# Attention with grouped keys: scores computed keys-first, exp read straight from PSUM, row sums checked on the chip

## The chip, the core and the metric

The kernel runs on one core of a Trainium2 chip. The metric is the device time of one execution in microseconds (us). A core has five engines that run their own instruction streams and meet at semaphores: PE (TensorE, matrix multiply; "PEld" is its weight load), DVE (VectorE), ACT (ScalarE), POOL (GpSimd) and SP (SyncE, which here only issues DMAs). Matmuls write to PSUM, 8 banks of 512 f32 values per partition; everything else works in SBUF.

## The reference

```python
B, Hq, Hkv, Sq, Sk, D = 16, 32, 8, 288, 512, 128     # q, k, v: bfloat16, normal * 0.05
k = jnp.repeat(k, rep, axis=1)                        # rep = Hq // Hkv = 4
v = jnp.repeat(v, rep, axis=1)
scores = jnp.einsum("bhqd,bhkd->bhqk", q, k) * D ** -0.5
p = softmax(scores, axis=-1)
out = jnp.einsum("bhqk,bhkd->bhqd", p, v)             # (16, 32, 288, 128) bfloat16
```

Four query heads share one key head, so for each of the 16 x 8 = 128 pairs of batch and key head (a "group" here) there are 4 x 288 = 1152 query rows against the same 512 keys. Inputs are 16.8 MB of k, 16.8 MB of v and 37.7 MB of q; the output has 37.7 MB.

## The kernel before

The 1152 query rows of a group are cut into 9 units of 128 rows; there are 1152 units in all. A unit goes through these steps:

- `op_s` (L229, PE): one matmul, the unit's 128 queries as weights, the group's 512 keys streamed, into one bank of `ps_s` (three banks in turn). Queries lie on partitions, keys along the row.
- `op_dve` (L242, DVE): multiplies the scores by minus the scale into `sn_sb` (f32, SBUF) and takes the row minimum into `nmx_sb`, which is minus the row maximum.
- `op_pool` (L254, POOL): negates and adds that, so that the row maximum becomes 0; the result `x_sb` is bfloat16.
- `op_xt` (L271, PE): four 128 x 128 transposes of `x_sb` into `ps_x` (two units per buffer), so that keys come onto partitions, as the next matmul needs them.
- `op_exp` (L289, ACT): exp of two units at a time, 1024 values per partition, from `ps_x` into `pt_sb` (bfloat16).
- `op_pv` (L315, PE): four matmuls accumulate the unit's output: `pt_sb` as weights, `v_sb` streamed with 129 columns. Column 129 of `v_sb` is ones, so it yields the row sum. Three units share one bank of `ps_o` (two banks in turn).
- `op_rc` (L334, DVE): reciprocals of three row sums, `rl_sb`.
- `op_oev` (L376 on DVE, L385 on ACT): the scaled output of three units to `o_sb`. One in five goes to DVE as one instruction, the others to ACT as three.

The order on each engine is written out by hand: each step of unit u gets a due time (u, u + 1, u + 3 and so on, with lags `LAG_XT` = 3 and `LAG_PV` = 8), and each engine's list is sorted by it. SP issues the DMAs batch by batch (`op_load_qk`, `op_load_v`, `op_store`): a DMA transpose of q, a wait for it, one of k, a wait for it, then v, with two buffers; the first batch is loaded in two halves. The output of a batch is stored with one DMA, that of the last batch in four. In the store each row of 128 values (256 bytes) is a piece of its own, because row c x 128 + p of a group lies on partition p.

Of the kernel before, what the change touches and what calls it, by code (L numbers as in the profile page):

```python
# [6 lines left out]
ACTF = mybir.ActivationFunctionType  # L7
CFG = {}
BF16 = mybir.dt.bfloat16
FP32 = mybir.dt.float32  # L10


def bass_standalone__gqa_softmax__near_ridge_kernel(
# [8 lines left out]
    rep = Hq // Hkv  # L22
    P = 128
    assert D == P and Sk % P == 0 and (rep * Sq) % P == 0
    NJ = Sk // P
    NT = (rep * Sq) // P
    G = Hkv
    NG = B * G
    U = NG * NT
    UPB = G * NT  # L30
    FREE = NJ * P
    assert FREE * 4 <= 2048
    scale = float(D) ** -0.5
    DV = D + 1
    OPB = 2048 // (DV * 4)
    assert OPB >= 1 and NT % OPB == 0

    q_v = q.rearrange("b h s d -> b (h s) d")
    k_v = k.rearrange("b g s d -> b (g s) d")
    o_v = out.rearrange("b h s d -> b (h s) d").rearrange("b (c p) d -> b p c d", p=P)  # L40
    v_v = v.rearrange("b g s d -> b (g s) d").rearrange("b (c p) d -> b p c d", p=P)

    NSB = CFG.get('NSB', 3)
    NXB = CFG.get('NXB', 3)
    NS = CFG.get('NS', 3)
    NX = CFG.get('NX', 4)
    NPB = CFG.get('NPB', 4)
    NM = 8
    NR = 2
    XPB = CFG.get('XPB', 2)  # L50
    assert NS >= NSB and NSB + NXB * ((XPB + 1) // 2) + 2 <= 8
    LAG_XT = CFG.get('LAG_XT', 3.0)
    LAG_PV = CFG.get('LAG_PV', 8.0)
    OE_PERIOD = CFG.get('OE_PERIOD', 5)
    OE_DVE = CFG.get('OE_DVE', (2,))

    n_xc = (U + XPB - 1) // XPB
    n_oc = (U + OPB - 1) // OPB

    def xc_units(c):  # L60
        return list(range(c * XPB, min(U, (c + 1) * XPB)))

    def oc_units(r):
        return list(range(r * OPB, min(U, (r + 1) * OPB)))

    with ExitStack() as es:  # L66
        block = es.enter_context(nc.Block())
        v_sb = es.enter_context(nc.sbuf_tensor("v_sb", [P, 2, G, NJ, DV], BF16))
        o_sb = es.enter_context(nc.sbuf_tensor("o_sb", [P, 2, G, NT, D], BF16))
        qt_sb = es.enter_context(nc.sbuf_tensor("qt_sb", [P, 2, G, NT, P], BF16))  # L70
        kt_sb = es.enter_context(nc.sbuf_tensor("kt_sb", [P, 2, G, NJ, P], BF16))
        scr_sb = es.enter_context(nc.sbuf_tensor("scr_sb", [P, 16], FP32))
        sn_sb = es.enter_context(nc.sbuf_tensor("sn_sb", [P, NS, FREE], FP32))
        x_sb = es.enter_context(nc.sbuf_tensor("x_sb", [P, NX, FREE], BF16))
        pt_sb = es.enter_context(nc.sbuf_tensor("pt_sb", [P, NPB, XPB, NJ, P], BF16))
        nmx_sb = es.enter_context(nc.sbuf_tensor("nmx_sb", [P, NM], FP32))
        rl_sb = es.enter_context(nc.sbuf_tensor("rl_sb", [P, NR, OPB], FP32))
        ident = es.enter_context(nc.sbuf_tensor("ident", [P, P], BF16))
        ones_sb = es.enter_context(nc.sbuf_tensor("ones_sb", [P, P], BF16))
        ps_s = es.enter_context(nc.psum_tensor("ps_s", [P, NSB, FREE], FP32))  # L80
        ps_x = es.enter_context(nc.psum_tensor("ps_x", [P, NXB, XPB, NJ, P], BF16))
        ps_o = es.enter_context(nc.psum_tensor("ps_o", [P, 2, 512], FP32))
        class Chan:

            def __init__(self, name, n):
                self.n = n
                self.sems = [es.enter_context(nc.semaphore("%s%d" % (name, i))) for i in range(n)]

            def w(self, i, mult=1):
                return (self.sems[i % self.n], (i // self.n + 1) * mult)  # L90

            def s(self, i):
                return self.sems[i % self.n]

        c_ldq = Chan("ldq", 2)
        c_ldk = Chan("ldk", 2)
        c_ldv = Chan("ldv", 2)
        c_qkfree = Chan("qkfree", 2)
        c_vfree = Chan("vfree", 2)
        c_out = Chan("outd", 2)  # L100
        c_s = Chan("s", NSB)
        c_dve = Chan("dve", NS)
        c_pool = Chan("pool", max(NS, NX))
        c_xt = Chan("xt", NX)
        c_xc = Chan("xc", NXB)
        c_exp = Chan("exp", max(NPB, NXB))
        c_pv = Chan("pv", max(XPB * (NPB - 1) + 1, OPB + 1))
        c_rc = Chan("rc", NR)
        c_oev = Chan("oev", 2)
        c_osta = Chan("osta", 2)  # L110
        c_ostd = Chan("ostd", 2)
        s_init = es.enter_context(nc.semaphore("s_init"))
        s_q0a = es.enter_context(nc.semaphore("s_q0a"))
        s_pca = [es.enter_context(nc.semaphore("s_pca%d" % i)) for i in range(3)]
        s_pcd = [es.enter_context(nc.semaphore("s_pcd%d" % i)) for i in range(3)]
        s_k0a = es.enter_context(nc.semaphore("s_k0a"))
        s_c0 = es.enter_context(nc.semaphore("s_c0"))

        def emit(eng, waits, fn):
            waits = [(s, n) for (s, n) in waits if n > 0]  # L120
            for (s, n) in waits[:-1]:
                eng.wait_ge(s, n)  # L122
            ins = fn()
            if waits:
                s, n = waits[-1]
                ins.wait_op(s, n, "sem-ge")
            return ins

        def grp_of(u):
            return u // NT  # L130

        def bat_of_group(g):
            return g // G

        pe_pending = []

        def pe_carry(ins):
            if pe_pending:
                ins.then_inc(pe_pending.pop(0), 1)

        sp_plain = []

        def sp_drain():
            for (s, n) in sp_plain:
                nc.sync.wait_ge(s, n)
            del sp_plain[:]

        GH = G // 2 if G >= 2 else 0

        def op_load_qk(b, part=None):  # L150
            eng = nc.sync
            bb = b % 2
            sp_drain()
            if b >= 2:
                eng.wait_ge(*c_qkfree.w(b - 2))
            if part is None:
                g0, g1 = 0, G
            elif part == 0:
                g0, g1 = 0, GH
            else:  # L160
                g0, g1 = GH, G
            sq = s_q0a if part == 0 else c_ldq.s(b)
            sk = s_k0a if part == 0 else c_ldk.s(b)
            nq = 16 if part == 0 else c_ldq.w(b, 16)[1]
            nk = 16 if part == 0 else c_ldk.w(b, 16)[1]
            eng.dma_start_transpose(
                qt_sb[:, bb, g0:g1].rearrange("d g t p -> d (g t p)"),
                q_v[b, g0 * NT * P:g1 * NT * P]).then_inc(sq, 16)
            eng.wait_ge(sq, nq)
            eng.dma_start_transpose(  # L170
                kt_sb[:, bb, g0:g1].rearrange("d g j p -> d (g j p)"),
                k_v[b, g0 * NJ * P:g1 * NJ * P]).then_inc(sk, 16)
            eng.wait_ge(sk, nk)

        def op_load_v(b):
            eng = nc.sync
            bb = b % 2
            if b >= 2:
                eng.wait_ge(*c_vfree.w(b - 2))
            else:  # L180
                eng.wait_ge(s_init, 1)
            eng.dma_start(  # L182
                v_sb[:, bb].rearrange("p g j e -> p (g j) e")[:, :, 0:D], v_v[b]).then_inc(c_ldv.s(b), 16)
            sp_plain.append(c_ldv.w(b, 16))

        NPC = 4 if G % 4 == 0 else 1
        GPP = G // NPC

        def op_store(b, piece=None):
            eng = nc.sync  # L190
            bb = b % 2
            if piece is None or piece == NPC - 1:
                if n_oev_act[b]:
                    eng.wait_ge(*c_osta.w(b))
                if n_oev_dve[b]:
                    eng.wait_ge(*c_ostd.w(b))
            else:
                if piece_has[(False, piece)]:
                    eng.wait_ge(s_pca[piece], 1)
                if piece_has[(True, piece)]:  # L200
                    eng.wait_ge(s_pcd[piece], 1)
            if piece is None:
                g0, g1 = 0, G
            else:
                g0, g1 = piece * GPP, (piece + 1) * GPP
            eng.dma_start(
                o_v[b, :, g0 * NT:g1 * NT],
                o_sb[:, bb, g0:g1].rearrange("p g t d -> p (g t) d")).then_inc(c_out.s(b), 16)
            if piece is None:
                sp_plain.append(c_out.w(b, 16))  # L210

        def op_s(u):
            eng = nc.tensor
            g = grp_of(u)
            b = bat_of_group(g)
            bb = b % 2
            gl = g % G
# [289 lines left out]
```

## Time and profile before

| | |
|---|---|
| time, median of 3 runs | 829.54 us (829.42 to 829.66) |
| profiled execution: span from the first to the last instruction | 828.8 us |
| busy: PE, DVE, ACT, POOL | 96%, 96%, 95%, 94% of the span |
| granted TensorE clock, mean | 0.998 |
| DMA: moved, mean busy share of the 16 DMA engines (queue of SP) | 109.06 MB, 63.5% |
| HBM read and written by the instructions' own account | 16.78 MB and 37.75 MB |

The profile comes from one execution, with a record of each instruction. Its own time is the span, 0.7 us below the median of the runs. "Busy" is the time in which at least one instruction of the engine was in work; matmuls overlap in the records, so the pace of PE is better read from the starts of consecutive matmuls than from their lengths. A group's row has its busy time, the mean length of one instruction in ns, and the idle time of the engine just before such instructions with what ended it.

### The profile page before, as it was taken

The numbers are of one execution on the slowest core, as the hardware profiler recorded it, in microseconds if no ns is written. First come the engines' busy times: TensorE is split into PE (matmuls) and PEld (weight loads), VectorE is DVE, ScalarE is ACT, GpSimd is POOL, SyncE is SP. The second block draws the span as 40 slices with busy tenths as digits, with TensorE's granted clock in tenths as the row PEclk, the third lists the DMA queues.
The fourth block names the chain that finished last, engine by engine and source line by source line (L and its number), as shares of the span: only waits on it lengthen the run. The fifth ranks groups of instructions, "written<-read, shape, count | busy, mean of one in ns | idle before, by whom it ended". The sixth has DMA issues, their size and how long they took to land.

```text
span 828.8 us, 30229 instructions
## 1 busy us (share of the span) xinstructions
PE 791.8 (96%) x10177; PEld 643.5 (78%) x10368; DVE 795.6 (96%) x2786; ACT 786.2 (95%) x1517; POOL 778.9 (94%) x1157
## 2 busy tenths in 40 slices
PE   3999999999999999999999999999999999999996
PEld 1778878878888788778788788787888888787785
DVE  3999999999999999999999999999999999999995
ACT  2999999999999999999999999999999999999997
POOL 3999999999999999999999999999999999999995
PEclk9999999999999999999999999999999999999999
DMA  6868758297691857848387573876919569383522
GB/s 133 162 140 168 167 116 170 51 173 159 116 217 34 184 119 153 181 75 176 85 167 167 114 154 72 172 158 117 214 28 196 115 132 202 85 161 90 116 59 59
DMA packets 378633, 111.00 MB, mean 134 GB/s; under 512 B 362096, under 2 KB 378480, under 8 KB 378480
## 3 DMA queue, kind: packets, MB, share of 16 engines
q1 hardware_dynamic: 378480, 109.06, 63.5%
q8 instruction: 84, 1.38, 0.7%
q14 instruction: 69, 0.57, 0.2%
HBM read 16.78 MB, written 37.75 MB: 66 GB/s over the span
## 4 chain that ended last, share of the span: by engine, by line
PE 41%; ACT 39%; issue 17%; DMA 2%; ACTq 0%; DVE 0%; SPq 0%
ACT o_sb L385 22%; ACT pt_sb L289 17%; PE ps_o L315 15%; PE ps_x L271 14%; PE ps_s L229 11%; DMA v_sb<-in_v_dram 1%; DMA qt_sb<-in_q_dram 1%; DMA kt_sb<-in_k_dram 1%; ACT scr_sb L405 0%; ACTq L66 0%; DVE rl_sb L334 0%; ACTq L122 0%; SPq L182 0%
## 5 line engine op out<-in xcount | busy, mean ns | idle before, releaser
L254 POOL TENSOR_SCALAR x_sb<-sn_sb,nmx_sb 128x512 bf16<-128x512 f32 x1152 | 778.4, 698 | 39.9 <-DVE sn_sb L242 36.1
L242 DVE TENSOR_SCALAR_CACHE_REDUCE sn_sb<-ps_s 128x512 f32<-128x512 f32 x1152 | 756.4, 680 | 23.5 <-PE ps_s L229 22.0
L289 ACT ACTIVATE pt_sb<-ps_x 128x1024 bf16<-128x1024 bf16 x576 | 595.4, 1074 | 35.6 <-PE ps_x L271 27.5
L315 PE MATMUL ps_o<-v_sb,pt_sb 128*128 128x129 bf16 x4608 | 459.5, 221 | 9.4 <-ACT o_sb L385 2.3
L271 PE MATMUL ps_x<-ident,x_sb 128*128 128x128 bf16 x4608 | 445.6, 219 | 10.4 <-POOL x_sb L254 0.2
L271 PEld LDWEIGHTS ps_x<-ident,x_sb 128*128 128x128 bf16 x4608 | 324.9, 97 | 140.8 <-POOL x_sb L254 46.4
L229 PE MATMUL ps_s<-kt_sb,qt_sb 128*128 128x512 bf16 x961 | 363.9, 379 | 12.0 <-DMA kt_sb<-in_k_dram 12.0
L315 PEld LDWEIGHTS ps_o<-v_sb,pt_sb 128*128 128x128 bf16 x4608 | 306.3, 98 | 25.9 <-ACT o_sb L385 20.6
L385 ACT ACTIVATE o_sb<-ps_o,rl_sb 128x128 bf16<-128x128 f32 x921 | 283.3, 413 | 1.2 <-DVE rl_sb L334 1.2
L229 PEld LDWEIGHTS ps_s<-kt_sb,qt_sb 128*128 128x128 bf16 x1152 | 113.4, 98 | 13.1 <-DMA kt_sb<-in_k_dram 12.0
L242 DVE DVE_READ_ACCUMULATOR sn_sb<-ps_s 128x1 f32 x1152 | 95.7, 83 | 0.0
L334 DVE RECIPROCAL rl_sb<-ps_o 128x3 f32<-128x3 f32 x384 | 67.4, 176 | 3.6 <-PE ps_o L315 3.6
L376 DVE TENSOR_TENSOR o_sb<-ps_o,rl_sb 128x384 bf16<-128x384 f32 x77 | 42.6, 553 | 0.0
L405 ACT ACTIVATE scr_sb<-ones_sb 128x1 f32<-128x1 bf16 x16 | 4.3, 271 | 0.0
L289 ACT ACT_TABLE_LOAD x1 | 1.3, 1283 | 1.8 <-POOL ident L443 1.8
L443 POOL TENSOR_SCALAR_AFFINE_SELECT ident<-ones_sb 128x128 bf16<-128x128 bf16 x1 | 0.3, 295 | 0.9 <-DVE v_sb L470 0.9
L469 DVE MEMSET ones_sb<- 128x128 bf16 x1 | 0.2, 165 | 0.9 <-PEq L492 0.9
L403 DVE MEMSET scr_sb<- 128x1 f32 x16 | 0.9, 59 | 0.0
L400 ACT ACTIVATE scr_sb<-ones_sb 128x1 f32<-128x1 bf16 x3 | 0.9, 314 | 0.0
L492 POOL MEMSET const-float32-0.0<- 128x1 f32 x1 | 0.1, 99 | 0.3 <-issue 0.3
L470 DVE MEMSET v_sb<- 128x64 bf16 x1 | 0.1, 112 | 0.2 <-issue 0.2
L398 DVE MEMSET scr_sb<- 128x1 f32 x3 | 0.2, 59 | 0.0
(3 smaller groups left out, 0.3 us busy)
## 6 DMA issues: line engine op xcount, KB each, us to landing
out_dram<-o_sb SPq DMA_DIRECT2D x15, 2304.0 KB, 15.5
out_dram<-o_sb SPq DMA_DIRECT2D x4, 576.0 KB, 3.5
qt_sb<-in_q_dram SPq DMA_TRANSPOSE x17, 12.2
kt_sb<-in_k_dram SPq DMA_TRANSPOSE x17, 6.8
v_sb<-in_v_dram SPq DMA_DIRECT2D x16, 0.2 KB, 7.5
```

What stands on the lines that cost most here:

```text
L229: emit(eng, waits, lambda: eng.matmul(ps_s[:, u % NSB, :], qt_sb[:, bb, gl, t, :], kt_sb[:, bb, gl].rearrange("p j c -> p (j c)"), start=T ...
L242: emit(eng, waits, lambda: eng.tensor_scalar(out=sn_sb[:, u % NS, :], in0=ps_s[:, u % NSB, :], scalar1=-scale, scalar2=None, op0=ALU.mult, ...
L254: emit(eng, waits, lambda: eng.tensor_scalar(out=x_sb[:, u % NX, :], in0=sn_sb[:, u % NS, :], scalar1=-1.0, scalar2=nmx_sb[:, u % NM:u % N ...
L271: ins = emit(eng, w, lambda: eng.transpose(ps_x[:, c % NXB, slot, j, :], x_sb[:, u % NX, j * P:(j + 1) * P], ident[:]))
L289: emit(eng, waits, lambda: eng.activation(pt_sb[:, c % NPB, 0:n].rearrange("p a j c -> p (a j c)"), ps_x[:, c % NXB, 0:n].rearrange("p a j ...
L315: ins = emit(eng, w, lambda: eng.matmul(ps_o[:, r % 2, oslot * DV:(oslot + 1) * DV], pt_sb[:, c % NPB, slot, j, :], v_sb[:, bb, gl, j, :], ...
L334: emit(eng, waits, lambda: eng.reciprocal(rl_sb[:, r % NR, 0:n], src.rearrange("p a e -> p (a e)"))).then_inc(c_rc.s(r), 1)
L376: emit(eng, waits, lambda: eng.tensor_tensor(out=o_sb[:, bb, gl, t0:t0 + n, :], in0=src_o, in1=rl_sb[:, r % NR, 0:n].unsqueeze(2).broadcas ...
L385: ins = emit(eng, w, lambda: eng.activation(o_sb[:, bb, gl, t0 + i, :], ps_o[:, r % 2, i * DV:i * DV + D], ACTF.Identity, scale=rl_sb[:, r ...
L400: nc.scalar.activation(scr_sb[:, 8 + pc:9 + pc], ones_sb[:, 0:1], ACTF.Identity).then_inc(s_pca[pc], 1)
L403: nc.vector.memset(scr_sb[:, b % 2:b % 2 + 1], 0.0).then_inc(c_ostd.s(b), 1)
L405: nc.scalar.activation(scr_sb[:, 4 + b % 2:5 + b % 2], ones_sb[:, 0:1], ACTF.Identity).then_inc(c_osta.s(b), 1)
```

## The change

The kernel is rewritten around chunks. A group's scores are 4 key blocks x 1152 query rows = 4608 columns with 128 keys on the partitions; they are cut into three chunks of 1536 columns, which is three PSUM banks. `ps_s` holds two chunks.

- `op_s(n)`: for chunk n, matmuls with a block of 128 keys as weights and queries streamed; cuts fall at bank borders and at ends of key blocks, so each chunk takes four matmuls (512, 512, 128, 384 columns in the first). The scores come out transposed.
- `op_exp(n)` (ACT): exp of the whole chunk from `ps_s` (f32) to `pt_sb`, with the scale folded in. No row maximum is subtracted.
- `op_pv(r)`: 12 matmuls for three output tiles. Tile t takes the query rows p x 9 + t, so the weights are read from `pt_sb` with a step of 9 elements.
- `op_rc`, `op_ev` (DVE): reciprocals, kept for the whole run in `rl_sb`, and all evictions.
- `op_stat` (DVE): once per batch, largest and smallest reciprocal. At the end these give a flag: 1 or more if a reciprocal is over 2^30 or under 2^-30. A one-column matmul adds the flags of all partitions, and each engine loads the result into a register.
- `general_path`: the old computation (with the row maximum, and evictions on DVE alone), emitted behind a branch that each engine takes if the register isn't zero.
- SP: loads in units of four groups with three slots, k before q, without waits between transposes; the first unit as one group and three. Stores per group, with 9 x 128 values (2304 bytes) in one piece per partition, from six buffers.

```diff
+    CB = 3
+    CH = CB * BANK          # 1536
+    LAG = NC + 1            # NC = 3 chunks a group
+    UG = 4
+    NSLOT = 3
+    NPT = 3
+    NO = 6
+    o_v = out.rearrange("b h s d -> (b h s) d").rearrange("(g p t) d -> g p (t d)", p=P, t=NT)
+        ps_s = main.enter_context(nc.psum_tensor("ps_s", [P, 2, CH], FP32))
+        ps_o = main.enter_context(nc.psum_tensor("ps_o", [P, 2, BANK], FP32))
...
+        def op_s(n):
...
+            if n >= 2:
+                waits.append(("s_e", n - 1))
+            ps = pieces(i)
+            for x, (a, b) in enumerate(ps):
+                j, r0 = a // R, a % R
+                ins = emit(eng, waits if x == 0 else [], lambda: eng.matmul(
+                    ps_s[:, n % 2, a - i * CH:b - i * CH],
+                    kt_sb[:, sl, gi, j * P:(j + 1) * P],
+                    qt_sb[:, sl, gi, r0:r0 + b - a], start=True, stop=True))
+            ins.then_inc(sem["s_s"], 1)
...
+        def op_pv(r):
...
+            waits = [("us_v%d" % sl, 16 * (u // NSLOT + 1)), ("s_e", NC * (g + 1))]
+            if r >= 2:
+                waits.append(("s_ev", r - 1))
+            for a in range(3):
+                t = 3 * (r % NC) + a
+                for j in range(NJ):
+                    w = pt_sb[:, g % NPT, j * R:(j + 1) * R].rearrange("k (p t) -> k t p", t=NT)[:, t]
+                    ins = emit(eng, waits if a == 0 and j == 0 else [], lambda: eng.matmul(
+                        ps_o[:, r % 2, a * DV:(a + 1) * DV], w,
+                        v_sb[:, sl, gi * NJ + j, 0:DV],
+                        start=(j == 0), stop=(j == NJ - 1)))
+            ins.then_inc(sem["s_pv"], 1)
...
+        def op_exp(n):
+            eng = nc.scalar
+            g, i = n // NC, n % NC
+            waits = [("s_s", n + 1)]
+            if g >= NPT:
+                waits.insert(0, ("s_pv", NC * (g - NPT + 1)))
             emit(eng, waits, lambda: eng.activation(
+                pt_sb[:, g % NPT, i * CH:(i + 1) * CH], ps_s[:, n % 2], ACTF.Exp, scale=scale)
+            ).then_inc(sem["s_e"], 1)
...
+        for u in range(1, NU):
+            sp.append((-8.0 if u < NSLOT else NC * UG * (u - NSLOT + 1) + LAG, lambda u=u: op_load(u)))
+        for g in range(NG):
+            sp.append((NC * (g + 1) + LAG + 1.5, lambda g=g: op_store(g)))
...
         @block.tensor
         def _(eng):
+            for n in range(NS + LAG):
+                if n < NS:
+                    op_s(n)
+                if n >= LAG:
+                    op_pv(n - LAG)
+            emit(eng, [("s_bad", 1)], lambda: eng.matmul(
+                ps_s[0:1, 0, 0:1], one_f[:], ck_sb[:, 3:4], start=True, stop=True)
+            ).then_inc(sem["s_bad"], 1)
...
+        def guarded(key, first=None):
+            def body(eng):
+                eng.wait_ge(sem["s_flag"], 1)
+                reg = eng.alloc_register("bad_" + key)
+                eng.load(reg, flag_i[:])
+                with eng.If_ne(reg, 0):
+                    if first:
+                        first(eng)
+                    fns[key](eng)
+            return body
```

More of the change, by code (lines that the diff above doesn't have):

```diff
@@ L48, in bass_standalone__gqa_softmax__near_ridge_kernel @@
[L48 to L64, printed above, removed]
@@ L66, in bass_standalone__gqa_softmax__near_ridge_kernel @@
-    with ExitStack() as es:
-        block = es.enter_context(nc.Block())
[L68 to L117, printed above, removed]
@@ new lines, in bass_standalone__gqa_softmax__near_ridge_kernel, with S, need @@
+    VP = 160
+    LAG = NC + 1
+    UG = 4
+    NU = NG // UG
+    NSLOT = 3
+    NPT = 3
+    NO = 6
+    q_v = q.rearrange("b h s d -> (b h s) d")
+    k_v = k.rearrange("b g s d -> (b g s) d")
+    v_v = v.rearrange("b g (j p) d -> p (b g j) d", p=P)
+    o_v = out.rearrange("b h s d -> (b h s) d").rearrange("(g p t) d -> g p (t d)", p=P, t=NT)
+    with ExitStack() as es:
+        sem = {}
+        def S(name):
+            if name not in sem:
+                sem[name] = es.enter_context(nc.semaphore(name))
+            return sem[name]
+        flag_i = es.enter_context(nc.sbuf_tensor("flag_i", [1, 1], I32))
+        block = es.enter_context(nc.Block())
+        main = ExitStack()
+        v_sb = main.enter_context(nc.sbuf_tensor("v_sb", [P, NSLOT, UG * NJ, VP], BF16))
+        qt_sb = main.enter_context(nc.sbuf_tensor("qt_sb", [P, NSLOT, UG, R], BF16))
+        kt_sb = main.enter_context(nc.sbuf_tensor("kt_sb", [P, NSLOT, UG, Sk], BF16))
+        pt_sb = main.enter_context(nc.sbuf_tensor("pt_sb", [P, NPT, COLS], BF16))
+        o_sb = main.enter_context(nc.sbuf_tensor("o_sb", [P, NO, NT, D], BF16))
+        rl_sb = main.enter_context(nc.sbuf_tensor("rl_sb", [P, NG * NT], FP32))
+        st_sb = main.enter_context(nc.sbuf_tensor("st_sb", [P, 2, B], FP32))
+        ck_sb = main.enter_context(nc.sbuf_tensor("ck_sb", [P, 4], FP32))
+        one_f = main.enter_context(nc.sbuf_tensor("one_f", [P, 1], FP32))
+        dum = main.enter_context(nc.sbuf_tensor("dum", [P, 2], FP32))
+        ps_s = main.enter_context(nc.psum_tensor("ps_s", [P, 2, CH], FP32))
+        ps_o = main.enter_context(nc.psum_tensor("ps_o", [P, 2, BANK], FP32))
+        seen = {}
+        def need(eng, waits):
+            left = []
+            for (s, n) in waits:
+                key = (id(eng), s)
+                if seen.get(key, 0) < n:
+                    seen[key] = n
+                    left.append((sem[s], n))
+            return left
@@ L119, in emit @@
         def emit(eng, waits, fn):
-            waits = [(s, n) for (s, n) in waits if n > 0]
+            waits = need(eng, waits)
             for (s, n) in waits[:-1]:
@@ L175, in op_load_v @@
[L175 to L210, printed above, removed]
@@ L295, in op_pv @@
[L295 to L323 removed]
+                ins.wait_op(waits[-1][0], waits[-1][1], "sem-ge")
@@ new lines, in op_store, with pieces @@
+        def op_store(g):
+            eng = nc.sync
+            for (s, n) in need(eng, [("s_ev", NC * (g + 1))]):
+                eng.wait_ge(s, n)
+            eng.dma_start(o_v[g], o_sb[:, g % NO].rearrange("p t d -> p (t d)")).then_inc(sem["s_o%d" % (g % NO)], 16)
+        def pieces(i):
+            cuts = sorted({i * CH, (i + 1) * CH}
+                          | {x for x in range(0, COLS, BANK) if i * CH < x < (i + 1) * CH}
+                          | {x for x in range(0, COLS, R) if i * CH < x < (i + 1) * CH})
+            return list(zip(cuts[:-1], cuts[1:]))
@@ L329, in op_rc @@
-            waits = []
-            if r >= NR:
-                waits.append(c_oev.w(r - NR))
-            waits.append(c_pv.w(us[-1]))
-            src = ps_o[:, r % 2, 0:n * DV].rearrange("p (a e) -> p a e", e=DV)[:, :, D:DV]
-            emit(eng, waits, lambda: eng.reciprocal(
-                rl_sb[:, r % NR, 0:n], src.rearrange("p a e -> p (a e)"))
-            ).then_inc(c_rc.s(r), 1)
-        obuf_waited = {(False, bq): False for bq in range(B)}
-        obuf_waited.update({(True, bq): False for bq in range(B)})
@@ L437, in bass_standalone__gqa_softmax__near_ridge_kernel @@
[L437 to L448 removed]
+            src = ps_o[:, r % 2, 0:3 * DV].rearrange("p (a e) -> p a e", e=DV)[:, :, D:DV]
@@ new lines, in op_rc, with op_ev @@
+            emit(eng, [("s_pv", r + 1)], lambda: eng.reciprocal(
+                rl_sb[:, 3 * r:3 * r + 3], src.rearrange("p a e -> p (a e)"))
+            ).then_inc(sem["s_rc"], 1)
+        def op_ev(r):
+            eng = nc.vector
+            g = r // NC
+            waits = [("s_rc", r + 1)]
+            if g >= NO:
+                waits.insert(0, ("s_o%d" % (g % NO), 16 * (g // NO)))
+            t0 = 3 * (r % NC)
+            src = ps_o[:, r % 2, 0:3 * DV].rearrange("p (a e) -> p a e", e=DV)[:, :, 0:D]
+            emit(eng, waits, lambda: eng.tensor_tensor(
+                out=o_sb[:, g % NO, t0:t0 + 3, :], in0=src,
+                in1=rl_sb[:, 3 * r:3 * r + 3].unsqueeze(2).broadcast_to([P, 3, D]),
+                op=ALU.mult)).then_inc(sem["s_ev"], 1)
```

621 lines of the change are left out of this document (339 added, 282 removed).

## The prediction

> **What bounds the kernel now.** I read the shares first, then the costliest groups, then the chain of waits, then single stretches of the timeline. The first two rows below are busy time by engine and the granted TensorE clock, the third is the chain that ended last, and the rest are groups (busy us, mean ns of one, idle before).
>
> ```profile
> PE 791.8 (96%) x10177; PEld 643.5 (78%) x10368; DVE 795.6 (96%) x2786; ACT 786.2 (95%) x1517; POOL 778.9 (94%) x1157
> PEclk9999999999999999999999999999999999999999
> PE 41%; ACT 39%; issue 17%; DMA 2%; ACTq 0%; DVE 0%; SPq 0%
> L254 POOL TENSOR_SCALAR x_sb<-sn_sb,nmx_sb 128x512 bf16<-128x512 f32 x1152 | 778.4, 698 | 39.9 <-DVE sn_sb L242 36.1
> L242 DVE TENSOR_SCALAR_CACHE_REDUCE sn_sb<-ps_s 128x512 f32<-128x512 f32 x1152 | 756.4, 680 | 23.5 <-PE ps_s L229 22.0
> L289 ACT ACTIVATE pt_sb<-ps_x 128x1024 bf16<-128x1024 bf16 x576 | 595.4, 1074 | 35.6 <-PE ps_x L271 27.5
> L271 PE MATMUL ps_x<-ident,x_sb 128*128 128x128 bf16 x4608 | 445.6, 219 | 10.4 <-POOL x_sb L254 0.2
> L315 PEld LDWEIGHTS ps_o<-v_sb,pt_sb 128*128 128x128 bf16 x4608 | 306.3, 98 | 25.9 <-ACT o_sb L385 20.6
> L385 ACT ACTIVATE o_sb<-ps_o,rl_sb 128x128 bf16<-128x128 f32 x921 | 283.3, 413 | 1.2 <-DVE rl_sb L334 1.2
> L334 DVE RECIPROCAL rl_sb<-ps_o 128x3 f32<-128x3 f32 x384 | 67.4, 176 | 3.6 <-PE ps_o L315 3.6
> L376 DVE TENSOR_TENSOR o_sb<-ps_o,rl_sb 128x384 bf16<-128x384 f32 x77 | 42.6, 553 | 0.0
> ```
>
> Five engines stand at 94 to 96%: no single one bounds the kernel, and an edit that relieved one would gain nothing. This edit relieves four. So the question is what is left to do per piece, on which engine it is longest, and at what pace. Matmul durations overlap in the records (219 ns each for 128 columns), so I take the pace from start to start. These timeline rows (start, length, engine, line, count) are from a full stretch and from the last one:
>
> ```profile
> 401.70 0.27 PEld L315 LDWEIGHTS ps_o<-v_sb,pt_sb 128*128 128x128 bf16 x4
> 401.75 0.40 PE L315 MATMUL ps_o<-v_sb,pt_sb 128*128 128x129 bf16 x4
> 401.99 0.38 PE L229 MATMUL ps_s<-kt_sb,qt_sb 128*128 128x512 bf16 x1
> 402.20 0.38 PE L271 MATMUL ps_x<-ident,x_sb 128*128 128x128 bf16 x4
> 402.43 0.40 PE L315 MATMUL ps_o<-v_sb,pt_sb 128*128 128x129 bf16 x4
> 822.68 0.88 PE L315 MATMUL ps_o<-v_sb,pt_sb 128*128 128x129 bf16 x12 [1.28 <-ACT o_sb L385]
> 399.77 0.92 ACT L385 ACTIVATE o_sb<-ps_o,rl_sb 128x128 bf16<-128x128 f32 x3
> 400.52 1.99 ACT L289 ACTIVATE pt_sb<-ps_x 128x1024 bf16<-128x1024 bf16 x2
> 402.33 0.96 ACT L385 ACTIVATE o_sb<-ps_o,rl_sb 128x128 bf16<-128x128 f32 x3
> ```
>
> The reader should take four paces from them. One 512-column score matmul: 401.99 to 402.20, 0.215 us. Four transposes: 402.20 to 402.43, 0.23 us, or 57 ns each. Four PV matmuls: 401.75 to 401.99, 0.24 us, about 58 ns each (the run of 12 gives (0.88 - 0.22)/11 = 60 ns). One exp of 1024: two start at 400.52 and the next group starts at 402.33, so 0.905 us; the evictions of 128 go at 0.25 us (399.77 to 400.52 for three). A weight load of 98 ns precedes each matmul, and the pace of 58 ns shows that it is hidden beside the matmuls.
>
> **The change, part by part.** There are 128 groups (batch times key head) of 9 x 128 query rows. After the change each group is three chunks of 1536 score columns (keys on partitions), so 384 chunks.
>
> Removed: DVE's scaling with the row minimum (L242), POOL's subtraction (L254) and the 36 transposes of a group. POOL is left with nothing. DVE keeps the reciprocal and takes all evictions: 384 x (0.176 + 0.553) = 280 us. That is half the time to come, and it runs beside PE with two ps_o banks, so I cost it at nothing; were it not hidden, each chunk would have 0.73 us more.
>
> PE per chunk: four score matmuls with 1536 columns, 3 x 0.215 plus a few ns for the fourth piece = 0.65 us; twelve PV matmuls of 129 columns, 12 x 58 ns = 0.70 us. Sum 1.35 us, 384 x 1.35 = 518 us.
>
> On the Trainium skill's page "TensorE: Matmul & The Clock Gate" (Back-to-back issue gap) the sustained pace of a load-and-matmul stream at 128 columns is about 81 ns. The trace's 58 ns contradicts it for contiguous weights; with 81 ns the chunk would be 0.65 + 0.97 = 1.62 us and the whole some 645 us.
>
> ACT per chunk: one exp of 1536 from PSUM instead of 1.5 of 1024, and no evictions. Its cost is not in the trace. From below: the step between 128 and 1024 elements, (0.905 - 0.25)/896 = 0.73 ns an element (too low, as the eviction also reads a per-row scale), gives 0.905 + 512 x 0.73 ns = 1.28 us. From above: proportional, 0.905 x 1.5 = 1.36 us. I take 1.32, the middle: 507 us. Reading f32 in place of bf16 from PSUM I cost at nothing, since the eviction reads f32. PE is thus longest by a hair.
>
> Does the new ring of waits hold the two back? Score chunk n+2 waits until exp n has emptied its half of ps_s, exp n+2 waits for score chunk n+2. One round: exp (1.32 plus the 0.17 by which a 1.07 record exceeds its pace) + scores 0.65 + matmul drain 0.16 (0.38 - 0.215) = 2.30 us plus two signals, against 2 x 1.35 = 2.70 for two chunks. About 0.2 us per signal is spare, so the ring is not the bound, but jitter will cost something. I put 1% on the steady part (5 us): the kernel before loses 4% of PE with five engines level, here two or three are.
>
> Weights of PV: they are now read with a step of 9 elements (18 bytes) in pt_sb, because query row p x 9 + t goes to partition p. No row of this trace has a stepped weight read. From below nothing (still hidden under 58 ns), from above the full recorded 98 ns without any cover: 12 x 98 = 1.18 us. I take nothing, as today's loads of 98 ns hide in a 58 ns pace; the upper end is a rival below.
>
> Start. These rows are the issue times on SP's queue and, from the chain in order of time, the landings:
>
> ```profile
> 0.80 4.75 SPq L166 DMA_TRANSPOSE qt_sb<-in_q_dram  x1
> 0.80 6.85 DMA qt_sb<-in_q_dram
> 7.66 2.01 SPq L170 DMA_TRANSPOSE kt_sb<-in_k_dram  x1
> 7.66 4.32 DMA kt_sb<-in_k_dram
> 12.06 7.66 DMA v_sb<-in_v_dram
> 12.03 2.01 PE L229 MATMUL ps_s<-kt_sb,qt_sb 128*128 128x512 bf16 x4 [12.03 <-DMA kt_sb<-in_k_dram]
> ```
>
> Issuing takes 1.0 ns a row (4608 rows in 4.75, 2048 in 2.01), landing 2.2 us more. The new first load is one group: 512 + 1152 rows, not waited for in between: 0.8 + 0.5 + 1.2 + 2.2 = 4.7 us to the first matmul, where it was 12.0. Then three groups more (5.1 us of issue) and V, half of the 1 MB that took 7.66 us: about 12.5 us until the first PV. By then PE can do five score chunks (3.2 us), so it idles 12.5 - 4.7 - 3.2 = 4.6 us.
>
> Loads and stores otherwise: a load of four groups now waits on SP for the PV of the slot's former owner, and stores queue behind it; they wait about 7 us of issue, and six o_sb buffers (6 x 4.05 us) cover that. Stores become one row of 2304 bytes per partition where they were 256-byte pieces. The DMA rows:
>
> ```profile
> q1 hardware_dynamic: 378480, 109.06, 63.5%
> out_dram<-o_sb SPq DMA_DIRECT2D x15, 2304.0 KB, 15.5
> out_dram<-o_sb SPq DMA_DIRECT2D x4, 576.0 KB, 3.5
> qt_sb<-in_q_dram SPq DMA_TRANSPOSE x17, 12.2
> kt_sb<-in_k_dram SPq DMA_TRANSPOSE x17, 6.8
> 364.00:378.00 14.00, 13.73 (x180) 10.70 (x184) 13.79 (x51) 13.88 (x30) 13.62 (x21) 1.00 0.92 170
> 385.00:401.00 16.00, 15.71 (x207) 12.87 (x209) 15.74 (x55) 15.79 (x33) 15.50 (x24) 1.00 0.98 216
> ```
>
> The transfers keep the 16 engines busy for 0.635 x 828.8 = 526 us. If stores of the new shape cost what they do now, DMA needs as long as PE; if they cost half, 526 - 16 x 15.5/2 = 402 us. I take the cheaper end, since each partition's piece is nine times as long, and cost DMA at nothing. The cover is thin: DMA then works 80% of the time.
>
> End. After the last exp three PV chunks remain, part of the 518 but behind a wait of about 0.4 us. The rest of the tail:
>
> ```profile
> 823.60 0.18 DVE L334 RECIPROCAL rl_sb<-ps_o 128x3 f32<-128x3 f32 x1 [1.38 <-PE ps_o L315]
> 821.65 0.56 DVE L376 TENSOR_TENSOR o_sb<-ps_o,rl_sb 128x384 bf16<-128x384 f32 x1
> 824.81 0.37 SPq L206 DMA_DIRECT2D out_dram<-o_sb  x1
> ```
>
> Reciprocal, eviction and two signals 1.2 us; the last store, half of the 576 KB that take 3.5 us, about 3. The check of the row sums (32 small reductions of DVE during the run, hidden; then two more, two tiny operations, a one-column matmul, a copy) runs beside the store. What follows does not: every engine waits for the flag, loads a register and jumps over the other program. No row shows a register load or a long jump; from below 0.2 us (what stands after the last landing now), from above, by the nearest fetches from memory, two landings of 3.5 us. I take 3.
>
> Sum: 4.7 + 4.6 + 518 + 5 + 0.4 + 1.2 + 3 + 3 = 540 us of span, where the profiled execution has 828.8; the median of the runs, 829.54, lies 0.7 above that span, so 541 us.
>
> **The rivals.** (1) *Stepped weights are no longer hidden.* For it: each of the 128 reads of a partition jumps 18 bytes; every load row before is contiguous. Against: nothing in rows. At 98 ns per PV matmul the chunk is 0.65 + 1.18 = 1.83 us: 384 x 1.83 + 22 = 725 us; at half way (78 ns) 632 us. The Trainium skill speaks for it: "SBUF — State Buffer" (Door 1, on cachelines) has lines of 16 bytes that need two hits each for full bandwidth, and 18 bytes never hit twice. It also speaks against: "TensorE: Matmul & The Clock Gate" (Weight-path perf modes) allows the fast load a column step up to 1024 elements. No run here shows either yet.
>
> (2) *The other side: slower than before.* The same place, but the load takes twice its present record and nothing covers it: 2 x 98 = 196 ns, chunk 3.0 us, some 1174 us. It decides from (829.5 - 22)/384 - 0.65 = 1.45 us for twelve, 121 ns per PV matmul.
>
> (3) *DMA becomes the bound.* For it: 526 us as they stand, and engines were busy only 0.92 to 0.98 of a stretch full of transfers. Unchanged stores give 526/0.95 + 12 = 566 us, with score matmuls waiting for kt_sb and qt_sb. Against: the long store rows, and loads issued some 20 chunks (27 us) ahead.
>
> (4) *The other program runs as well.* If the sums left the allowed range (2^-30 to 2^30), the old computation would follow: about 541 + 850 = 1390 us. The inputs are normal numbers times 0.05, so scores are near 0 and sums near 512. I give it under 1%.
>
> **How the numbers follow.** Forecast (PE pace, 524 to 560): 0.55. DMA bound (545 to 590): 0.14. Stepped weights (1), anywhere from 570 to 760: 0.26, of which a third is above 680. Slower, (2) and (4): 0.04. The remaining 0.01 is around no change; 0.2% is about what a measurement of this kernel can tell from no change. The low end 524 is paces at their floor (1.32 us a chunk, 507 + 17). The high end 680 leaves 0.04 + 0.09 + a few hundredths out. Faster 0.95, same 0.01, slower 0.04.
>
> **What would show it.** PE near 95%, ACT near 94%, POOL empty, DVE about half; three-chunk rhythm of 4.05 us a group; score matmuls still 0.215 us apart, PV 58 ns apart. If PV starts lie 70 ns or more apart while ACT idles behind PE, (1) is right. If PE's idle time ends with kt_sb or qt_sb landings and the DMA share is above 0.95, (3). If exp takes over 1.36 us from start to start, ACT is the bound and I mis-sized it. First matmul at about 5 us; the time from the last eviction's end to the end about 6 us.

## The result and the profile after

The changed kernel takes 542.37 us (542.26 to 542.77, 4 runs) against 829.56 us before on the same chip: a ratio of 0.6539, 95% interval 0.653 to 0.6548. The profiled execution spans 540.5 us. These are rows of its page: busy time by engine, the chain that ended last by engine, the costliest groups, the DMA queue and the stores.

```profile
PE 526.1 (97%) x6146; PEld 427.7 (79%) x6146; DVE 289.8 (54%) x808; ACT 523.3 (97%) x386; POOL 0.2 (0%) x4
PE 96%; DMA 1%; SPq 1%; DVE 1%; issue 0%
L460 ACT ACTIVATE pt_sb<-ps_s 128x1536 bf16<-128x1536 f32 x384 | 521.9, 1450 | 5.9 <-PE ps_s L429 5.8
L447 PEld LDWEIGHTS ps_o<-v_sb,pt_sb 128*128 128x128 bf16 x4608 | 333.2, 140 | 40.4 <-DMA v_sb<-in_v_dram 0.6
L429 PE MATMUL ps_s<-qt_sb,kt_sb 128*128 128x512 bf16 (+3 forms) x1536 | 315.2, 328 | 7.2 <-DMA qt_sb<-in_q_dram 7.0
L480 DVE TENSOR_TENSOR o_sb<-ps_o,rl_sb 128x384 bf16<-128x384 f32 x384 | 214.1, 557 | 13.5 <-DVE rl_sb L468 0.3
L468 DVE RECIPROCAL rl_sb<-ps_o 128x3 f32<-128x3 f32 x384 | 69.3, 181 | 230.8 <-PE ps_o L447 230.8
q1 hardware_dynamic: 299584, 109.07, 87.0%
out_dram<-o_sb SPq DMA_DIRECT2D x128, 288.0 KB, 4.3
```

POOL is empty and DVE is at half, as forecast. PE and ACT both stand at 97%, so the shares do not tell which of them sets the pace. The chain names PE (96%), but it also does so, with 95%, for a run below that goes at ACT's pace, so it does not decide either. The page also has a sign of the disputed step: a PV weight load is recorded with 140 ns, where the same load had 98 ns before. The rhythm is in the timeline of PE (start, length, engine, line, count):

```profile
300.16 0.81 PE L429 MATMUL ps_s<-qt_sb,kt_sb 128*128 128x384 bf16 x4
300.81 0.86 PE L447 MATMUL ps_o<-v_sb,pt_sb 128*128 128x129 bf16 x12
301.50 0.81 PE L429 MATMUL ps_s<-qt_sb,kt_sb 128*128 128x512 bf16 x4
302.15 0.86 PE L447 MATMUL ps_o<-v_sb,pt_sb 128*128 128x129 bf16 x12
302.85 0.81 PE L429 MATMUL ps_s<-qt_sb,kt_sb 128*128 128x512 bf16 x4
303.50 0.90 PE L447 MATMUL ps_o<-v_sb,pt_sb 128*128 128x129 bf16 x12
304.23 0.81 PE L429 MATMUL ps_s<-qt_sb,kt_sb 128*128 128x384 bf16 x4
```

A score block takes 0.65 us from its start to the next block (300.16 to 300.81), a PV block 0.69, 0.70 and 0.73 us. One group, 300.16 to 304.23, is 4.07 us (4.073 by the starts of its exps, 1.347, 1.347 and 1.379 us apart); 128 of them are 521 us.

Start and end, from the timeline:

```profile
0.80 1.23 SPq L388 DMA_TRANSPOSE kt_sb<-in_k_dram  x1
2.08 1.34 SPq L391 DMA_TRANSPOSE qt_sb<-in_q_dram  x1
5.78 2.74 PE L429 MATMUL ps_s<-qt_sb,kt_sb 128*128 128x512 bf16 x8 [5.78 <-DMA qt_sb<-in_q_dram]
8.79 1.46 PE L429 MATMUL ps_s<-qt_sb,kt_sb 128*128 128x384 bf16 x4 [0.26 <-ACT pt_sb L460]
11.43 2.72 PE L429 MATMUL ps_s<-qt_sb,kt_sb 128*128 128x512 bf16 x8 [1.18 <-DMA qt_sb<-in_q_dram]
14.05 1.01 PE L447 MATMUL ps_o<-v_sb,pt_sb 128*128 128x129 bf16 x12
533.71 0.56 DVE L480 TENSOR_TENSOR o_sb<-ps_o,rl_sb 128x384 bf16<-128x384 f32 x1
535.48 0.15 DVE L551 CAST flag_i<-ps_s 1x1 int32<-1x1 f32 x1 [0.28 <-PE ps_s L521]
```

The first matmul comes at 5.78 us, the first PV at 14.05, the last eviction ends at 534.27, the flag is there at 535.63, and the program ends at 540.5.

### The profile page after: what moved, and what is told of

Read it like the earlier page. It is cut to its first block, busy times and chain, and to the rows that moved or that the text cites. A ratio compares the mean times of both kernels' runs of the same rounds, so it can differ in the third digit from the quotient of the medians.

```text
span 540.5 us, 14095 instructions
## 1 busy us (share of the span) xinstructions
PE 526.1 (97%) x6146; PEld 427.7 (79%) x6146; DVE 289.8 (54%) x808; ACT 523.3 (97%) x386; POOL 0.2 (0%) x4
## 4 chain that ended last, share of the span: by engine, by line
PE 96%; DMA 1%; SPq 1%; DVE 1%; issue 0%
PE ps_o L447 50%; PE ps_s L429 46%; DMA qt_sb<-in_q_dram 1%; SPq L388 0%; DVE o_sb L480 0%; SPq L391 0%; DVE rl_sb L468 0%; PE ps_s L521 0%; DVE ck_sb L548 0%; DVE ck_sb L542 0%; DVE ck_sb L545 0%; DVE flag_i L551 0%; DVE st_sb L492 0%; DVE st_sb L490 0%; DVE ck_sb L544 0%
## 5 line engine op out<-in xcount | busy, mean ns | idle before, releaser
L460 ACT ACTIVATE pt_sb<-ps_s 128x1536 bf16<-128x1536 f32 x384 | 521.9, 1450 | 5.9 <-PE ps_s L429 5.8
L447 PEld LDWEIGHTS ps_o<-v_sb,pt_sb 128*128 128x128 bf16 x4608 | 333.2, 140 | 40.4 <-DMA v_sb<-in_v_dram 0.6
L447 PE MATMUL ps_o<-v_sb,pt_sb 128*128 128x129 bf16 x4608 | 334.7, 222 | 0.3 <-DVE o_sb L480 0.2
L429 PE MATMUL ps_s<-qt_sb,kt_sb 128*128 128x512 bf16 (+3 forms) x1536 | 315.2, 328 | 7.2 <-DMA qt_sb<-in_q_dram 7.0
L480 DVE TENSOR_TENSOR o_sb<-ps_o,rl_sb 128x384 bf16<-128x384 f32 x384 | 214.1, 557 | 13.5 <-DVE rl_sb L468 0.3
L468 DVE RECIPROCAL rl_sb<-ps_o 128x3 f32<-128x3 f32 x384 | 69.3, 181 | 230.8 <-PE ps_o L447 230.8
L429 PEld LDWEIGHTS ps_s<-qt_sb,kt_sb 128*128 128x128 bf16 x1536 | 131.6, 99 | 65.3 <-DMA qt_sb<-in_q_dram 5.8
L492 DVE TENSOR_REDUCE st_sb<-rl_sb 128x1 f32<-128x72 f32 x16 | 3.5, 218 | 0.0
L490 DVE TENSOR_REDUCE st_sb<-rl_sb 128x1 f32<-128x72 f32 x16 | 3.5, 217 | 0.0
L535 DVE MEMSET v_sb<- 128x1536 bf16 x1 | 1.3, 1338 | 0.3 <-issue 0.3
```

The costliest lines, as they stand in the source:

```text
L429: ins = emit(eng, waits if x == 0 else [], lambda: eng.matmul(ps_s[:, n % 2, a - i * CH:b - i * CH], kt_sb[:, sl, gi, j * P:(j + 1) * P], ...
L447: ins = emit(eng, waits if a == 0 and j == 0 else [], lambda: eng.matmul(ps_o[:, r % 2, a * DV:(a + 1) * DV], w, v_sb[:, sl, gi * NJ + j, ...
L460: emit(eng, waits, lambda: eng.activation(pt_sb[:, g % NPT, i * CH:(i + 1) * CH], ps_s[:, n % 2], ACTF.Exp, scale=scale)).then_inc(sem["s_ ...
L468: emit(eng, [("s_pv", r + 1)], lambda: eng.reciprocal(rl_sb[:, 3 * r:3 * r + 3], src.rearrange("p a e -> p (a e)"))).then_inc(sem["s_rc"], 1)
L480: emit(eng, waits, lambda: eng.tensor_tensor(out=o_sb[:, g % NO, t0:t0 + 3, :], in0=src, in1=rl_sb[:, 3 * r:3 * r + 3].unsqueeze(2).broadc ...
L490: emit(eng, [("s_rc", (b + 1) * w // 3)], lambda: eng.tensor_reduce(st_sb[:, 0, b:b + 1], rl_sb[:, b * w:(b + 1) * w], AX.X, ALU.max))
```

## Experiments

Theory 1, held at first because exps followed each other at a seemingly fixed 1.347 us: ACT sets the pace. Its rival, theory 2: PE does, and ACT waits for each score chunk. Times below are medians; the kernel before took 829.7 to 830.5 us on these chips.

**Less work on PE.**

```diff
-                for j in range(NJ):
+                for j in range(NJ - 1):
...
-                        start=(j == 0), stop=(j == NJ - 1)))
+                        start=(j == 0), stop=(j == NJ - 2)))
```

> Each output tile adds up three of the four key blocks, so the fourth block's share is left out of the sums: 9 PV matmuls a chunk in place of 12, PE 1.17 us a chunk in place of 1.345. The exp is the same. If ACT sets the pace (1.347 us from exp to exp, a hair over PE), the time stays at 542 us within 3 us, and exp starts stay 1.346 to 1.347 apart. If PE sets it, the exps come closer, to what ACT can do alone (1.33 us by the exp of 1024 before), some 6 us or more off: 536 or below.

536.5 us (ratio 0.6466, 0.6456 to 0.6476): 5.9 us faster, so theory 1 falls. PE's timeline now has 9 PV matmuls a block, but a block still lasts 0.68 us:

```profile
300.88 0.82 PE L429 MATMUL ps_s<-qt_sb,kt_sb 128*128 128x384 bf16 x4
301.54 0.68 PE L447 MATMUL ps_o<-v_sb,pt_sb 128*128 128x129 bf16 x9
302.23 0.82 PE L429 MATMUL ps_s<-qt_sb,kt_sb 128*128 128x512 bf16 x4
303.57 0.61 PE L429 MATMUL ps_s<-qt_sb,kt_sb 128*128 128x512 bf16 x3
```

Two chunks from 300.88 to 303.57 are 2.69 us (the exps start 1.343 us apart), though a quarter of the PV work is gone. That is ACT's own pace, as the runs below bear out: the next limit lies only 1% below PE's 4.07/3 = 1.357 us. My 1.33 us for it was too low.

**Less work on ACT.**

```diff
-                pt_sb[:, g % NPT, i * CH:(i + 1) * CH], ps_s[:, n % 2], ACTF.Exp, scale=scale)
+                pt_sb[:, g % NPT, i * CH:i * CH + 1408], ps_s[:, n % 2, 0:1408], ACTF.Exp, scale=scale)
...
+            eng.memset(pt_sb[:].rearrange("p n (i c) -> p (n i) c", c=CH)[:, :, 1408:CH], 1.0)
```

> The exp is taken over 1408 of each chunk's 1536 columns; the last 128 of each chunk are left as ones. PE's work is the same. ACT a chunk falls by about 128 x 0.83 = 107 ns to 1.24 us. If ACT alone sets the pace, the time falls by about 384 x 0.107 = 41 us; if PE is within a hair of it, it stops at PE's own 1.345 us and the time falls by 1 to 5 us only (the two 1.347 us intervals hardly move, the third of 1.379 goes to 1.345).

541.98 us (0.6531, 0.6521 to 0.6541): no gain that can be told from none, where I had expected 1 to 5 us; the third interval did not shrink. The exp's record is 107 ns shorter, and PE's timeline is unchanged:

```profile
L460 ACT ACTIVATE pt_sb<-ps_s 128x1408 bf16<-128x1408 f32 x384 | 515.7, 1343 | 11.1 <-PE ps_s L429 5.6
300.51 0.81 PE L429 MATMUL ps_s<-qt_sb,kt_sb 128*128 128x384 bf16 x4
301.16 0.86 PE L447 MATMUL ps_o<-v_sb,pt_sb 128*128 128x129 bf16 x12
301.86 0.81 PE L429 MATMUL ps_s<-qt_sb,kt_sb 128*128 128x512 bf16 x4
```

Scores to PV 0.65, PV to scores 0.70, as in the changed kernel. So PE sets the pace: theory 2.

**The wait that ACT has once a group.**

```diff
             waits = [("s_s", n + 1)]
-            if g >= NPT:
-                waits.insert(0, ("s_pv", NC * (g - NPT + 1)))
```

> ACT's extra wait once a group, for the PV that last read the group's part of pt_sb, is dropped: PE has finished that PV before the score chunk whose signal the exp waits for anyway. Every third exp interval is 1.379 us now and 1.347 the others. Theory: that wait, an instruction of its own on ACT, costs 33 ns; without it all intervals are 1.347 and the time falls by 128 x 33 ns = 4.2 us to 538. Rival: the 33 ns are PE's (its PV block is 731 ns in place of 695 once a group), and the time stays.

542.33 us (0.6536, 0.6527 to 0.6545): nothing, so the rival holds. Every third interval stays long with the wait gone (1.347, 1.347, 1.379 us); it is the PV block of 0.73 us on PE. Why one block in three is slower I did not settle; it goes with the step of the weights, below.

**Weights without a step, short stores.** Query row t x 128 + p on partition p, as in the kernel before.

```diff
-    ...rearrange("(g p t) d -> g p (t d)", p=P, t=NT)
+    ...rearrange("(g t p) d -> g p t d", p=P, t=NT)
...
-                    w = pt_sb[:, g % NPT, j * R:(j + 1) * R].rearrange("k (p t) -> k t p", t=NT)[:, t]
+                    w = pt_sb[:, g % NPT, j * R + t * P:j * R + (t + 1) * P]
```

> Query row t x 128 + p goes to partition p as in the kernel before: the PV weights are read without a step and the stores are 256-byte pieces again. DMA's busy time rises from 470 us to about 470 + 65 = 535 us (stores took 166 us of the engines before and take 101 now). If the third rival's mechanism is real, DMA becomes the bound and PE waits for kt_sb and qt_sb: 555 to 575 us. If transfers stay hidden up to a full share, 542 us.

536.81 us (0.6471, 0.6461 to 0.6481): faster, where I had expected the same or slower. Rows of its page, of PE's timeline and one exp of ACT's:

```profile
L447 PEld LDWEIGHTS ps_o<-v_sb,pt_sb 128*128 128x128 bf16 x4608 | 292.5, 98 | 56.1 <-DVE o_sb L480 1.1
q1 hardware_dynamic: 430656, 109.07, 102.9%
300.74 0.82 PE L429 MATMUL ps_s<-qt_sb,kt_sb 128*128 128x384 bf16 x4
301.40 0.84 PE L447 MATMUL ps_o<-v_sb,pt_sb 128*128 128x129 bf16 x12
302.09 0.82 PE L429 MATMUL ps_s<-qt_sb,kt_sb 128*128 128x512 bf16 x4
303.43 0.82 PE L429 MATMUL ps_s<-qt_sb,kt_sb 128*128 128x512 bf16 x4
300.26 1.77 ACT L460 ACTIVATE pt_sb<-ps_s 128x1536 bf16<-128x1536 f32 x1
```

Loads are at 98 ns again, and the kernel runs at ACT's pace: two chunks are 2.69 us (300.74 to 303.43), as with a quarter of the PV work gone. Who waits for whom shows in one gap. The exp above ends at 302.03, and the score block that needs its half of `ps_s` starts at 302.09, 0.06 us later: PE was waiting. In the changed kernel this gap is 0.39 us:

```profile
301.01 1.45 ACT L460 ACTIVATE pt_sb<-ps_s 128x1536 bf16<-128x1536 f32 x1
```

It ends at 302.46, and the score block in question starts at 302.85. The ring of waits is not what makes 1.343 us. With the 1.45 us that an exp takes when it does not queue, one round is 1.45 + 0.04 + 0.82 + 0.06 = 2.37 us (exp, start of the next exp after its scores, scores, gap), or 1.19 a chunk.

The DMA queue's packets add up to 1.03 times the 16 engines' span (they overlap in the records) and no wait came of it.

**Weights without a step, long stores.**

```diff
-                    w = pt_sb[:, g % NPT, j * R:(j + 1) * R].rearrange("k (p t) -> k t p", t=NT)[:, t]
+                    w = pt_sb[:, g % NPT, j * R + t * P:j * R + (t + 1) * P]
```

> Only the weight step goes: tile t takes the query columns t x 128 to t x 128 + 127 of pt_sb without a step, and the long stores stay, so that output rows land in another order within a group. The kernel with unstepped weights and short stores took 536.8 us, with ACT's exps 1.343 us apart and DMA busy at a full share. Theory A (the step of the weights is the 5.5 us, transfers are hidden either way): 536.8 within 1 us. Theory B (short stores at a full DMA share cost something that the missing step more than paid for): 2 us or more below 536.8.

537.17 us (0.6474, 0.6465 to 0.6483), the same as with short stores: theory A. The step of the weights costs the 5.5 us, the shape of the stores costs nothing in either form.

**The load's own pace.** With 33 columns streamed a matmul no longer covers its load.

```diff
-                        ps_o[:, r % 2, a * DV:(a + 1) * DV], w,
-                        v_sb[:, sl, gi * NJ + j, 0:DV],
+                        ps_o[:, r % 2, (a + 1) * DV - 33:(a + 1) * DV], w,
+                        v_sb[:, sl, gi * NJ + j, DV - 33:DV],
...
+            eng.memset(ps_o[:], 1.0)
```

> PV matmuls stream only the last 33 of v_sb's 129 columns (31 to 32 output columns and the row sum; the rest of ps_o stays at ones), so most of the output is left out and a matmul no longer covers its weight load. The starts of PV matmuls then show the load's own pace with a step of 9 elements. If the load of the step costs 41 ns more than without (138 against 98 ns recorded), its pace is some 41 ns longer than in the run without a step; by the 57 to 60 ns seen with 129 columns it should be just under or around 57 ns. Time: ACT's pace, about 537.

> The same 33 columns with weights read without a step (output rows in another order as well). If loads without a step are far from binding, PV starts lie 15 to 30 ns apart, against about 57 with the step; if the step costs nothing, both are alike. Time: ACT's pace, about 537.

536.6 us with the step and 535.13 without, one run each. The first two rows are from the run with the step (groups, then timeline), the next fence has the same from the run without:

```profile
L447 PEld LDWEIGHTS ps_o<-v_sb,pt_sb 128*128 128x128 bf16 x4608 | 336.5, 156 | 41.7 <-DMA v_sb<-in_v_dram 1.6
301.38 0.85 PE L447 MATMUL ps_o<-v_sb,pt_sb 128*128 128x33 bf16 x12
```

```profile
L447 PEld LDWEIGHTS ps_o<-v_sb,pt_sb 128*128 128x128 bf16 x4608 | 171.9, 96 | 58.0 <-DVE o_sb L480 2.1
300.85 0.46 PE L447 MATMUL ps_o<-v_sb,pt_sb 128*128 128x33 bf16 x12
```

Twelve matmuls in 0.85 us, the last one's own 0.21 taken off, are (0.85 - 0.21)/11 = 58 ns apart with the step; without it (0.46 - 0.18)/11 = 25 ns. The 58 is an average: in the trace the first interval is 28 ns and those from the third matmul on are 60 ns. So a stepped load needs 60 ns and a plain one at most 25. A matmul of 129 columns takes 56 to 57 ns with plain weights: it covers the plain load twice and the stepped one just not. This is why the step costs a few per cent of PV and not a multiple.

The Trainium skill bears on it in "SBUF — State Buffer" (Door 1, cachelines): lines of 16 bytes need two hits for full bandwidth, so a step of 18 bytes pays. The two paces, 25 and 60 ns, agree with its direction; it has no figure for the loss.

**The check and the second program.** Left out from the last reductions on; the branch and `general_path` too.

```diff
-            emit(eng, [("s_bad", 1)], lambda: eng.matmul(
...
-        fns = general_path(nc, gen, q, k, v, out, sem["s_go"])
```

> The check at the end (last reductions, flag, register loads) and the branch with the whole second program are left out; the per-batch reductions stay. The changed kernel's tail after the last eviction is 6.2 us, of which 3.7 us is PE's branch over the second program. The last store lands 2.2 us after that eviction. So the end is then set by the store: 542.4 - 3.4 = 539 us. Rival: the jump is free because something else at the program's end waits as long: 542.

538.48 us (0.6489, 0.6479 to 0.6498): the check at the end, with the branch, costs 4 us, 0.7% of the kernel.

**The kernel before without the row maximum.** The other part of the change, keys on partitions, is not made here; exp moves to the front, and DVE copies in its place.

```diff
+            emit(eng, waits, lambda: eng.activation(
+                x_sb[:, u % NX, :], ps_s[:, u % NSB, :], ACTF.Exp, scale=scale)
...
-            emit(eng, waits, lambda: eng.activation(
+            emit(eng, waits, lambda: eng.tensor_copy(
                 pt_sb[:, c % NPB, 0:n].rearrange("p a j c -> p (a j c)"),
-                ps_x[:, c % NXB, 0:n].rearrange("p a j c -> p (a j c)"),
-                ACTF.Exp)
+                ps_x[:, c % NXB, 0:n].rearrange("p a j c -> p (a j c)"))
```

> The kernel before, with one part of the change alone: no row maximum. ACT takes exp straight from ps_s (512 columns, f32) into x_sb, POOL does nothing, the transposes stay, and DVE copies ps_x to pt_sb where it scaled before; two in five evictions are on DVE. PE keeps its 0.68 us a unit. Theory (transposes on PE were what held the kernel, the maximum came along): 1152 x 0.68 + 20 = 800 us, at most some 30 of the 287 us. Rival (the maximum's two passes were the cost): below 700 us.

801.43 us (0.9656, 0.9642 to 0.9671). Busy times and chain of its page:

```profile
PE 780.4 (98%) x10368; PEld 641.2 (80%) x10368; DVE 526.4 (66%) x1134; ACT 767.4 (96%) x1865; POOL 0.5 (0%) x5
PE 97%; DMA 2%; ACT 0%; issue 0%; DVE 0%; ACTq 0%; SPq 0%
```

POOL is empty and DVE has a third to spare, but PE holds the kernel at 801. Dropping the maximum alone is worth 28 of the 287 us. The rest needs the scores keys-first: the transposes take 0.23 us of PE's 0.68 us a unit, 1152 x 0.23 = 265 us. Keys-first scores with the maximum kept were not run.

**Towards a faster version.** Without step and extra wait, what is left above the pace is the start and the end; I tried the start. First, group by group (k, q, v of one group, then of the next):

```diff
...
-        sp.append((-10.0, lambda: op_load(0, 0)))
-        sp.append((-9.0, lambda: op_load(0, 1)))
+        for i in range(UG):
+            sp.append((-10.0 + 0.1 * i, lambda i=i: op_load(0, i)))
```

> Unstepped weights with short stores, without ACT's extra wait, and the first unit loaded group by group (k, q and v of one group, then of the next). ACT then sets the pace at 1.343 us. ACT idles 7.28 us at the start and 1.4 us until the fourth chunk's queries land; the second should go, the first stays: 536.8 - 1.4 = 535.4 us, and up to 2 us less if PE's late start (first PV at 14 us) also delays the end. Rival: twelve small loads at the start take SP as long as before, and the time stays at 536.8.

537.77 us (0.6482, 0.6473 to 0.6491): not faster than the 536.8 us with plain weights alone. ACT's timeline, first of the changed kernel, then of this one:

```profile
7.28 2.79 ACT L460 ACTIVATE pt_sb<-ps_s 128x1536 bf16<-128x1536 f32 x2 [4.46 <-PE ps_s L429]
10.29 1.45 ACT L460 ACTIVATE pt_sb<-ps_s 128x1536 bf16<-128x1536 f32 x1 [0.21 <-PE ps_s L429]
12.91 47.84 ACT L460 ACTIVATE pt_sb<-ps_s 128x1536 bf16<-128x1536 f32 x35 [1.17 <-PE ps_s L429]
```

```profile
10.01 13.54 ACT L459 ACTIVATE pt_sb<-ps_s 128x1536 bf16<-128x1536 f32 x10 [0.21 <-PE ps_s L430]
25.45 5.48 ACT L459 ACTIVATE pt_sb<-ps_s 128x1536 bf16<-128x1536 f32 x4 [1.91 <-PE ps_s L430]
```

The wait of 1.17 us went and one of 1.91 us took its place at the second unit, whose loads SP issued 4 us later. Then three parts (first group, second group, then v and the last two groups), with short stores:

> Unstepped weights, short stores and no extra wait on ACT, and the first unit in three parts: k and q of the first group, k and q of the second, v of all four, then k and q of the last two. In the version with twelve small loads the 1.2 us wait before the fourth chunk went, and 2.1 us came back at chunk 12, since SP was 4 us later with the second unit. Here SP is about 1 us later, which the second unit's slack should take. Theory: the wait goes and nothing comes back, 1 to 1.5 us under the version with unstepped weights: 535.5 us. Rival: the start's waits only move again: 537.

> The changed kernel once more on the same chip, for a comparison run for run: 542 to 543 us.

535.92 us (0.6455, 0.6446 to 0.6464) beside 542.45 us (0.6536, 0.6527 to 0.6545) for the changed kernel on the same chip. ACT then works from 7.29 us on without the second wait:

```profile
7.29 54.15 ACT L460 ACTIVATE pt_sb<-ps_s 128x1536 bf16<-128x1536 f32 x40 [4.47 <-PE ps_s L431]
```

This version beats both kernels, 6.5 us under the changed one and with the check kept. Most of it is the missing step; the 0.9 us under the run with plain weights and short stores, on another chip, is too little to count as shown.

## Why the prediction was right, and where it was not

541 forecast, 542.4 measured. The mechanism of the main term held: PE's matmul paces, not shares, gave the time. That the sum came out within 0.3% is in part luck, since several terms were wrong in ways that cancelled. Term by term, in us of span:

| term | forecast | measured |
|---|---|---|
| to the first matmul | 4.7 | 5.8 |
| until the first PV, beyond five score chunks at 0.65 | 4.6 | 5.0 (14.05 - 5.78 - 5 x 0.65) |
| 384 chunks, with jitter | 518 + 5 | 521.3 (128 x 4.073) |
| what is left up to the last eviction's end | 0.4 + 1.2 | 2.1 |
| last store, flag, jump | 3 + 3 | 6.2 |

- *Start.* The first matmul came 1.1 us late, mostly because the 512 rows of k took 1.23 us to issue and not the 0.5 us of 1.0 ns a row. PE then did not sit idle for 4.6 us: its waits were 0.26 and 1.18 us, and the score matmuls ran at half pace (two chunks in 2.74 us, starts of 512-column ones 0.43 us apart). The prediction's own row of the kernel before, four of them in 2.01 us, points the same way. V landed as PE got there, at about 14.0 us (forecast 12.5; its weight load waited 0.59 us for it), so a faster PE would have waited for V, and the size of the term held while most of what filled it was something else. Why the first matmuls are slow no run here shows.
- *Steady part.* Scores 0.65, as forecast; PV 0.69 to 0.73 for 0.70. The 5 us of jitter were a name for something else: the third PV block of each group, 0.73, regular to the last.
- *Stepped weights at nothing.* This step failed, in a small way. Unstepped PV blocks last 0.68 us, so the step costs PE some 9 us (0.69 + 0.70 + 0.73 against 3 x 0.683, times 128), of which 5.5 show before ACT takes over. Two other terms hid this: 58 ns a PV matmul, taken from the kernel before, is 1 ns above the 57 that plain weights need here (384 x 12 x 1 ns = 5 us), and the jitter added another 5. Rival 1's mechanism is thus real, but its price was wrong: I put the recorded 98 ns in place of the pace, which is 25 ns for plain loads and 60 ns for these; nor would the sign that I had named for it, PV starts 70 ns apart, have found it. A record's length is no pace; I had said so of matmuls and not applied it to loads. The Trainium skill's rule in "SBUF — State Buffer" (Door 1, cachelines) was right to be weighed, and its statement on the column step in "TensorE: Matmul & The Clock Gate" (Weight-path perf modes) was no protection against it.
- *The pace rule* of the Trainium skill's "TensorE: Matmul & The Clock Gate" (Back-to-back issue gap; 81 ns at 128 columns) is contradicted by both kernels' traces: 57 ns here with plain weights and 58 to 61 with the step.
- *ACT at 1.32.* It is 1.343 (range given: 1.28 to 1.36). "PE by a hair" came out right with both terms 0.01 to 0.02 higher, but only through the step that I had put at nothing: with plain weights PE needs about 0.65 + 0.68 = 1.33 us, and ACT is the longer.
- *DMA at 402 us.* Measured 0.87 x 540.5 = 470. The stores' saving was mis-sized: 526 fell by 56, not by 124; I had halved 15.5 us from issue to landing, which is no busy time. The conclusion stood for another reason: with unstepped weights the share went to 1.03 and nothing waited, so rival 3 is out, with its 566 us.
- *The end.* The check costs 4 us against 3, between its bounds 0.2 and 7. But I had put the register load and the jump behind the last store, 3 + 3, and they run beside it: without the check the kernel ends 2.6 us after the last eviction, with it 6.2. The sum of 6 was right by luck.
- *Rivals 2 and 4, slower than before.* The flag stayed zero, and 60 ns a load is far from the 121 ns that decides.

## What to carry to other kernels

Take the pace from starts in a dense stretch, per engine and per piece of work left, and sum that; shares of busy time say little when several engines stand level. To see which of two sets the pace, look at the gap between the end of one's work and the start of the other's that waits for it (0.06 us against 0.39 here). When an operand is read with a step, price the load by its own pace (stream fewer columns, and read the starts), not by its recorded length, and look whether the matmul in front still covers it. If it just does not, reordering rows to spare the stores can cost more than the stores did: here short stores were free.

## What the runs showed of the hardware that I had not expected

- A weight load with a step of 18 bytes runs at 60 ns, a plain one at 25 ns or less; their records say 156 and 96 ns in the runs with 33 columns.
- DMA engines at a summed share of 1.03 with 256-byte stores held up nothing, and stores of 2304 bytes per partition saved no time of the kernel.
- The exp of 1536 f32 values from three PSUM banks settles at 1.343 us when ACT sets the pace, and its record grows from 1450 to 1751 ns in that case. The trace shows where the growth comes from: an exp's record starts 0.04 us after its scores are done, whether ACT is free or not. With plain weights that is 0.42 us before the exp ahead of it ends, in the changed kernel 0.07 to 0.10, so the longer record holds waiting.
